# Scores head by head, the first head's mask on ScalarE, an earlier spread: one edit in a fused attention and expert kernel

## The chip, the cores and the metric

The kernel runs on one core of a Trainium2 chip. The metric is the device time of one execution in microseconds (us). Five engines work side by side, each through its own queue in program order: PE (TensorE, matrix products, whose weight loads are shown as PEld), DVE (VectorE), ACT (ScalarE), POOL (GpSimd) and SP (SyncE, which here only issues transfers). They wait for one another through semaphores.

## The reference

Attention with a threshold, then a two-layer expert, in float32:

```
scores = scale * q @ k^T                      # 8 batches x 8 heads, 576 x 576, head size 64
thresh = max(scores, axis=-1) - tau           # tau = 0.02
scores = where(scores >= thresh, scores, -1e9)
attn   = exp(scores - max); attn /= sum(attn) + 1e-9
x      = (attn @ v), heads side by side       # 4608 x 512
out    = leaky(x @ w_in) @ w_out              # leaky(h) = max(0.01 h, h); 512 -> 2048 -> 512
```

Every row of scores is needed with its maximum before anything of it can be masked, and all eight heads of a batch are needed before the expert can use a token.

## The kernel before, in words

Two heads of one batch make a pair (32 pairs), two pairs make a chunk `c` (16 chunks, two to a batch). A chunk has nine steps `t`: in steps 0 to 7 one tile of 128 queries against all 576 keys, for the two heads h = 0 and 1 of a pair; in step 8 the remaining 64 queries of both pairs. The order of all instructions is written out by hand in one loop over `c` and `t` (lines 403 to 468), and each engine executes its own in that order.

A step does the following.

- `s_mm` (L160): the scores of both heads, in PSUM, as a sum of three products of fp16 halves (hi hi, lo hi, hi lo), each in two halves of 288 keys: 12 matmuls. Head 0 uses rows 0 to 63 of the array, head 1 rows 64 to 127, and the two heads take turns. There are two PSUM buffers `s`, one for each head, so the scores of a head in the next step wait until DVE has read those of this step.
- `s_max`, once for each head (L183 to L206): DVE copies the negated scores to `sn` and takes their minimum `nmx`; POOL adds tau, which gives the threshold `nth`; ACT then does one of two things. Without `direct` it takes the exponent `e` (L193), which needs only `nmx`, and DVE masks `e` by the threshold one step later in `s_mask` (L216). With `direct` ACT masks by itself, in two instructions: `far` (L199), which needs `nth`, and `W` (L203).
- `s_mask` of the step before (L216 for each head that ACT did not mask), followed by a transposing transfer of the two weight rows on SP's queue (L222).

Around this, some steps carry more. In steps 6, 7, 8 and 0 `prep` transposes the q or k of a pair to come (L132, five matmuls into the PSUM buffer `A`), ACT copies them to fp16 `hi` (L140), and DVE makes the remainder `lo` (L141) as the last thing of the step, since it stands in the list `soon`. Between the two `s_max` of a step stand half of the step's expert units and the `prep`. After chunk c, the sums of its rows are turned into reciprocals (`sums_0` to `sums_3`, steps 0 and 1), spread over the partitions for each of its two pairs (`sums_4`: L265 into `A`, copied by ACT to `rc`, L270) and used on the product with v (`values`: 20 matmuls L281 into `A`; the product `xT`, L291, is again the last thing of DVE's step). `A` is one buffer.

The expert is cut into units of about the same size: 16 hidden units (four matmuls, L303, then ACT's `gM`, L307) and 16 parts of the output (four matmuls, L318; after every fourth ACT copies `osb`, L325) for a batch, and eight more for the last 64 tokens of two batches. `push_main` and `push_tail` put them in a list once a batch's `xT` are there; each step takes some from it: about 2.1 on average, weighted by `share[t]` over the nine steps, the fractions being carried over. A credit cannot exceed what is in the list. In chunks 0, 1 and most of 2 the list is empty; later it also runs out for two or three steps in chunks 4, 8 and 12. "The expert stage" below means everything from the first push on. The list's last 34 units are done after the loop.

POOL's queue carries, besides the thresholds, the transfers of v (5 at a time) and of the expert's weights. SP's queue carries the loads of q and k, the transposing transfers and the stores.

The line that decides who masks is in the loop:

```
direct = tau_f <= 16.0 and (
    t not in (3, 7) if c < 3 else t in (3, 5) or not any(u[0] for u in units[:n]))
s_max(c, t, 0, False)
...
s_max(c, t, 1, direct)
```

Of the kernel before, what the change touches and what calls it, by code (L numbers as in the profile page):

```python
# [16 lines left out]
def kernel(  # L17
# [52 lines left out]
    def bank():  # L70
        return ps.tile([128, 512], FP32, tag="u", bufs=2, name="u")

    def load_qk(p, i, tail):

        b, g = divmod(p, NG)
        if p not in nat:
            nat[p] = sb.tile([128, 9, 2, 64], FP32, tag="nat", bufs=3, name="nat")
        t = nat[p]
        h2 = (q, k)[i][b, 2 * g:2 * g + 2, :, :]
        if not tail:  # L80
            nc.sync.dma_start(
                out=t[0:128, 4 * i:4 * i + 4, :, :],
                in_=h2[:, 0:512, :].rearrange("h (p c) d -> p c h d", c=4),
            )
        else:
            nc.sync.dma_start(
                out=t[ds(64 * i, 64), 8, :, :],
                in_=h2[:, 512:576, :].rearrange("h p d -> p h d"),
            )
# [54 lines left out]
        ))  # L144
        qk.setdefault(p, {})[i] = (hi, lo)

    def s_mm(c, t):


        out = [ps.tile([128, 2, 512], FP32, tag="s", bufs=2, name="s") for _ in range(2)]  # L150
        if t < 8:
            srcs = [(2 * c + t // 4, ds(t % 4 * 128, 128), ds(0, 128))]
        else:
            srcs = [(2 * c + e, ds(512, 64), ds(64 * e, 64)) for e in range(2)]
        for half in range(2):
            for ti, (a, b) in enumerate(((0, 0), (1, 0), (0, 1))):
                for p, cols, po in srcs:
                    for h in range(2):
                        r = ds(h * 64, 64)
                        nc.tensor.matmul(  # L160
                            out=out[h][po, half, 0:288], lhsT=qk[p][0][a][r, cols],
                            rhs=qk[p][1][b][r, ds(half * 288, 288)],
                            start=(ti == 0), stop=(ti == 2), skip_group_check=True,
                        )
        sc[(c, t)] = out

    live, dens = {}, {}
# [86 lines left out]
    def sums_4(c, e):  # L254

        row = rows[c]
        t = pair_of_banks().rearrange("p a b -> p (a b)")

        if e == 0:
            parts = [(2 * s, s * 128, 0, 128) for s in range(4)] + [(16, 512, 0, 64)]  # L260
        else:
            parts = [(16, 0, 64, 64)] + [(8 + 2 * s, 64 + s * 128, 0, 128) for s in range(3)]
            parts += [(14, 448, 0, 64), (14, 512, 64, 64)]
        for i, q0, r0, n in parts:
            nc.tensor.matmul(  # L265
                out=t[:, ds(q0, n)], lhsT=sel[:, i:i + 2, :].rearrange("r i m -> r (i m)"),
                rhs=row[:, ds(r0, n)], start=True, stop=True, skip_group_check=True,
            )
        rc = sb.tile([128, 576], FP32, tag="rc", bufs=2, name="rc")
        nc.scalar.activation(out=rc[:, :], in_=t[:, 0:576], func=AF.Copy, bias=0.0, scale=1.0)  # L270
        rcs[e] = rc

    def values(c, e):

        b, g = divmod(2 * c + e, NG)
        wT, vb = wTs[c], Vs[b % 2]
        t = pair_of_banks()
        for half in range(2):
            for kb in range(5):
                for h in range(2):  # L280
                    nc.tensor.matmul(  # L281
                        out=t[ds(h * 64, 64), half, 0:288], lhsT=vb[:, g, h, kb, :],
                        rhs=wT[:, 4 * h + kb, ds(e * 576 + half * 288, 288)],
                        start=(kb == 0), stop=(kb == 4), skip_group_check=True,
                    )
        rc = rcs.pop(e)
        x = sb.tile([128, 576], FP16, tag=f"xT{g}", bufs=2, name=f"xT{g}")
        xTs[(b, g)] = x

        def mul():  # L290
            nc.vector.tensor_tensor(  # L291
                out=x.rearrange("p (a b) -> p a b", a=2), in0=t[:, :, 0:288],
                in1=rc.rearrange("p (a b) -> p a b", a=2), op=OP.mult,
            )
            nc.gpsimd.tensor_copy(out=xE[g][:, b, :], in_=x[:, 0:64] if e else x[:, 512:576])
        soon.append(mul)
# [76 lines left out]
            units.pop(0)[1]()  # L373

    with tc.manual_schedule():
        nc.scalar.preload_act_table_set("natural_log_exp_and_others")
        for i, tail in ((0, 0), (0, 1), (1, 1), (1, 0)):
            load_qk(0, i, tail)
        make_identity(nc, I32[:, 0:128])
        nc.vector.tensor_copy(out=I32[:, 128:192], in_=I32[:, 0:64])  # L380
        nc.vector.tensor_copy(out=I16[:, :], in_=I32[:, 0:128])
        nc.vector.memset(ntau[:, :], -tau_f)
        nc.vector.memset(r2[:, :, :], 0.0)
        nc.vector.tensor_tensor(
            out=sel[:, :, :], in0=I32[:, 0:18].unsqueeze(2).to_broadcast([128, 18, 64]),
            in1=I32[:, 64:82].unsqueeze(2).to_broadcast([128, 18, 64]), op=OP.add,
        )
        nc.vector.tensor_scalar(out=sel[:, :, :], in0=sel[:, :, :], scalar1=RS, scalar2=None, op0=OP.mult)
        for t in Vs:
            nc.vector.memset(t[64:128, :, 0, 4, :], 0.0)  # L390
            nc.vector.memset(t[0:64, :, 1, 0, :], 0.0)
        for p in range(1, 3):
            for i in range(2):
                for tail in range(2):
                    load_qk(p, i, tail)
        prep(0, 0)
        prep(0, 1, "s", 2)
        run(take(soon))
        share = (23, 27, 23, 13, 23, 13, 23, 23, 23)
        credit = 0.0  # L400
        w_at = [1 + 87 * i // 100 for i in range(32)]
        prev = None
        for c in range(NC + 1):
            last = c == NC
            for t in range(NT):
                step = c * NT + t
                if step == 1:
                    load_v(0)
                if c % 2 == 1 and t == 4 and c // 2 + 1 < B:
                    load_v(c // 2 + 1)  # L410
                for i in range(32):
                    if w_at[i] == step:
                        load_w(i)
                if c > 1 and c % 2 == 0 and t == 6:
                    push_main(c // 2 - 1)
                    if c % 4 == 0:
                        push_tail(c // 2 - 2)
                if not last:
                    s_mm(c, t)


                nxt = {6: (2 * c + 2, 0), 7: (2 * c + 2, 1), 8: (2 * c + 3, 0), 0: (2 * c + 1, 1)}
                if c == 0:
                    nxt[0], nxt[1] = (1, 0), (1, 1)
                pi = nxt.get(t)
                if pi is not None and pi[0] >= NP:
                    pi = None
                if c == 0 and t < 2:
                    prep(*pi)
                    pi = None  # L430

                if c > 0 and t in (3, 5):
                    values(c - 1, t // 2 - 1)
                credit = min(credit + 2.1 * 9 * share[t] / sum(share), len(units))
                n = int(credit)
# [69 lines left out]
```

## Time and profile before

| what | value |
|---|---|
| three runs | 554.84, 555.18 (median), 555.84 us |
| the profiled execution: its own time / its span | 553.93 us / 552.2 us |
| PE, DVE, ACT, POOL busy | 506.5, 423.1, 435.1, 183.4 us |
| mean granted clock of PE | 0.966 |
| DVE's first `sn` / that of chunk 3 / that of the last step | 10.86 / 96.62 / 498.47 us |
| DVE's copy of one head's scores (L183), 288 times | mean 752 ns |
| DVE's mask (L216), 196 times | mean 815 ns |
| ACT's exponent (L193), 196 times | mean 770 ns |
| ACT's own mask (L199 and L203), 92 times | mean 771 and 775 ns |
| POOL's threshold (L188), 288 times | mean 429 ns |

A page of the profile gives busy time by engine, then the span in 40 slices, where each digit is a busy share in tenths (PEclk is the clock granted to PE, in tenths of full speed). An instruction's duration covers its filling and emptying, so two in a row on one engine start closer together than a duration: where DVE works without a break, its copies of scores start 0.67 to 0.69 us apart. In the lists in order of time a line has its start, its length, engine, source line, operation, tiles out<-in, shapes, count, and in brackets the idle time of the engine before it with what ended that idle time.

### The profile page before, as it was taken

How to read it: one execution, taken by the hardware profiler on the slowest of the kernel's cores; microseconds unless marked ns; L12 is line 12 of the kernel's file. 1: busy time of each engine (PE TensorE's matmuls, PEld its weight loads, DVE VectorE, ACT ScalarE, POOL GpSimd, SP SyncE). 2: the span in 40 equal slices, each digit the busy share in tenths (PEclk: the TensorE clock that was granted, in tenths of full speed). 3: DMA queues.
4: the chain of work that ended last, by engine and by line, in shares of the span. 5: the costliest groups of instructions: out<-in, count | busy, mean ns of one | idle time of the engine just before them, and what ended most of it. 6: DMA issues, size and time to landing. Idle time of an engine off the chain costs nothing.

```text
span 552.2 us, 12416 instructions
## 1 busy us (share of the span) xinstructions
PE 506.5 (92%) x4416; PEld 279.6 (51%) x4416; DVE 423.1 (77%) x1106; ACT 435.1 (79%) x765; POOL 183.4 (33%) x430
## 2 busy tenths in 40 slices
PE   5668689899989999999989999999989999999996
PEld 3345445455545565455545565455545565444444
DVE  4897878798898879888898878888897878893000
ACT  2886879888987998799886998799887898885522
POOL 1756454253324222242224222242223332231000
PEclk9686859999999999999999999999999999999999
DMA  6999999999877979799867987798766976564001
GB/s 147 165 222 184 166 203 186 147 138 202 165 136 121 190 141 165 127 163 179 161 134 122 188 159 129 138 172 179 170 125 107 199 145 127 84 103 109 39 38 58
DMA packets 266814, 80.52 MB, mean 146 GB/s; under 512 B 251904, under 2 KB 264192, under 8 KB 266752
## 3 DMA queue, kind: packets, MB, share of 16 engines
q1 hardware_dynamic: 249216, 70.81, 71.3%
q0 software_dynamic: 17536, 8.92, 13.7%
q8 instruction: 35, 0.57, 0.5%
q14 instruction: 27, 0.22, 0.1%
HBM read 36.70 MB, written 9.44 MB: 84 GB/s over the span
## 4 chain that ended last, share of the span: by engine, by line
PE 53%; ACT 23%; DVE 11%; issue 7%; DMA 3%; POOL 2%; SPq 0%; DVEq 0%; ACTq 0%; POOLq 0%
PE u L318 19%; PE s L160 13%; PE u L303 11%; ACT e L193 7%; DVE sn L183 7%; PE A L281 6%; ACT gM L307 4%; ACT far L199 4%; ACT W L203 4%; PE A L132 3%; ACT hi L140 2%; DVE W L216 2%; DMA wT<-W 1%; DMA out_dram<-osb 1%; POOL nth L188 1%
## 5 line engine op out<-in xcount | busy, mean ns | idle before, releaser
L183 DVE TENSOR_SCALAR_CACHE_REDUCE sn<-s 128x576 f32<-128x576 f32 x288 | 206.9, 752 | 49.6 <-PE s L160 48.3
L188 POOL TENSOR_SCALAR nth<-nmx 128x1 f32<-128x1 f32 x288 | 123.6, 429 | 260.2 <-DVE sn L183 234.3
L193 ACT ACTIVATE e<-sn,nmx 128x576 f16<-128x576 f32 x196 | 150.5, 770 | 34.9 <-DVE sn L183 29.5
L216 DVE SCALAR_TENSOR_TENSOR W<-sn,nth,e 128x576 f16<-128x576 f32 x196 | 155.7, 815 | 2.2 <-POOL nth L188 2.2
L303 PE MATMUL u<-xT,win 128*128 128x512 f16 x512 | 128.5, 380 | 8.6 <-ACT gM L307 7.8
L318 PE MATMUL u<-wout,gM 128*128 128x512 f16 x512 | 125.3, 380 | 0.0
L160 PE MATMUL s<-hi,hi 64*128 64x288 f16 (+1 forms) x640 | 99.7, 301 | 12.6 <-DVE sn L183 11.2
L160 PEld LDWEIGHTS <-hi 64*128 64x128 f16 (+1 forms) x1280 | 67.4, 100 | 69.8 <-issue 54.3
L160 PE MATMUL s<-hi,lo 64*128 64x288 f16 (+1 forms) x640 | 94.5, 297 | 0.0
L160 PE MATMUL s<-lo,hi 64*128 64x288 f16 (+1 forms) x640 | 94.3, 297 | 0.0
L303 PEld LDWEIGHTS <-win 128*128 128x128 f16 x768 | 59.3, 98 | 67.7 <-issue 31.0
L199 ACT ACTIVATE far<-sn,nth 128x576 f32<-128x576 f32 x92 | 70.9, 771 | 23.7 <-POOL nth L188 21.5
L307 ACT ACTIVATE gM<-u 128x512 f16<-128x512 f32 x128 | 74.2, 588 | 15.8 <-PE u L303 15.8
L203 ACT ACTIVATE W<-far,ntau 128x576 f16<-128x576 f32 x92 | 71.3, 775 | 3.0
L318 PEld LDWEIGHTS <-gM 128*128 128x128 f16 x512 | 45.3, 98 | 51.1 <-issue 10.8
L141 DVE SCALAR_TENSOR_TENSOR lo<-A,hi 128x576 f16<-128x576 f32 x63 | 47.7, 757 | 23.9 <-ACT hi L140 23.6
L132 PE MATMUL A<-I,nat 128*128 128x128 f32 x315 | 49.2, 291 | 11.3 <-DVE lo L141 5.7
L132 PEld LDWEIGHTS A<-I,nat 128*128 128x128 f32 x315 | 39.2, 149 | 27.2 <-DVE lo L141 11.9
L281 PE MATMUL A<-wT,V 128*64 128x288 f16 x640 | 47.9, 298 | 1.7 <-ACT rc L270 1.6
L140 ACT ACTIVATE hi<-A 128x576 f16<-128x576 f32 x63 | 40.4, 641 | 11.5 <-PE A L132 11.5
L281 PEld LDWEIGHTS <-V 128*64 128x64 f16 x640 | 35.6, 113 | 12.7 <-issue 8.7
L160 PEld LDWEIGHTS <-lo 64*128 64x128 f16 (+1 forms) x640 | 32.9, 100 | 15.0 <-issue 11.1
(42 smaller groups left out, 279.8 us busy)
## 6 DMA issues: line engine op xcount, KB each, us to landing
nat<-in_q_dram SPq DMA_DIRECT2D x32, 256.0 KB, 4.2
nat<-in_k_dram SPq DMA_DIRECT2D x32, 256.0 KB, 3.8
out_dram<-osb SPq DMA_DIRECT2D x16, 512.0 KB, 2.9
wT<-W SPq DMA_TRANSPOSE x144, 3.9
V<-in_v_dram POOLq DMA_DIRECT2D x8, 256.0 KB, 5.6
V<-in_v_dram POOLq DMA_DIRECT2D x16, 128.0 KB, 5.8
win<-in_moe_w_in_dram POOLq DMA_DIRECT2D x16, 128.0 KB, 4.8
wout<-in_moe_w_out_dram POOLq DMA_DIRECT2D x16, 128.0 KB, 4.5
```

The lines of the kernel that those rows point to most:

```text
L132: nc.tensor.matmul(out=pt[0:128, ds(c * 128, 128)], lhsT=t[0:128, 4 * i + c if c < 4 else 8, :, :].rearrange("p h d -> p (h d)"), rhs=I32[ ...
L160: nc.tensor.matmul(out=out[h][po, half, 0:288], lhsT=qk[p][0][a][r, cols], rhs=qk[p][1][b][r, ds(half * 288, 288)], start=(ti == 0), stop= ...
L183: nc.vector.tensor_scalar(out=sn[:, h, :].rearrange("p (a b) -> p a b", a=2), in0=s_[:, :, 0:288], scalar1=-BS, scalar2=None, op0=OP.mult, ...
L188: nc.gpsimd.tensor_scalar(out=nth[:, h:h + 1], in0=nmx[:, h:h + 1], scalar1=1.0, scalar2=tau_f, op0=OP.mult, op1=OP.add,)
L193: nc.scalar.activation(out=e[:, h, :], in_=sn[:, h, :], func=AF.Exp, bias=nmx[:, h:h + 1], scale=-1.0,)
L199: nc.scalar.activation(out=far[:, :], in_=sn[:, h, :], func=AF.Prelu, bias=nth[:, h:h + 1], scale=-1.0, alpha=BIG,)
L203: nc.scalar.activation(out=w[:, ds(h * 576, 576)], in_=far[:, :], func=AF.Exp, bias=ntau[:, 0:1], scale=1.0, accum_out=dens[c][:, 2 * t + ...
L216: nc.vector.scalar_tensor_tensor(out=w[:, ds(h * 576, 576)], in0=sn[:, h, :], scalar=nth[:, h:h + 1], in1=e[:, h, :], op0=OP.is_le, op1=OP ...
L281: nc.tensor.matmul(out=t[ds(h * 64, 64), half, 0:288], lhsT=vb[:, g, h, kb, :], rhs=wT[:, 4 * h + kb, ds(e * 576 + half * 288, 288)], star ...
L303: nc.tensor.matmul(out=t[:, ts(j, N)], lhsT=w_in16[:, gi, ts(j0 + j, 128)], rhs=xs[gi], start=(gi == 0), stop=(gi == NG - 1), skip_group_c ...
L307: nc.scalar.activation(out=g_out, in_=t[:, 0:nj * N].rearrange("p (j n) -> p j n", j=nj), func=AF.Prelu, bias=0.0, scale=1.0, alpha=0.01)
L318: nc.tensor.matmul(out=t[:, :], lhsT=g_in(j), rhs=w_out16[:, j, :], start=(j == 0), stop=(j == NJ - 1), skip_group_check=True,)
```

## The change

There are five edits.

1. `s_mm` gets a flag `apart`, set when the list of units is empty at the step's start. Then all six products of head 0 come before the six of head 1; otherwise the order stays as it was.
2. `direct` now holds for head 0 instead of head 1, so ACT's queue has `far`, `W` before the units' copies and before `hi`, and `e` of head 1 after them. The steps in which ACT masks change too: in chunks 0 to 2 all but steps 2 and 7 (they were all but 3 and 7); later steps 3 and 4, and the others but step 2 if no hidden unit is among the step's units. Over the kernel that makes 87 steps with a mask on ACT (before: 92).
3. Both spreads of a chunk's sums are made in step 2 (they were made in steps 2 and 4), the second after the step's units; `values` comes in steps 3 and 4 (before: 3 and 5), behind the first half of the units.
4. The units are pushed in step 5 of an even chunk (before: 6), and `share` moves weight from steps 2 and 4 to step 5.
5. The large load of k for the first pair is issued on ACT's queue, as its first instruction. It was the fourth on SP's.

```
-        for half in range(2):
-            for ti, (a, b) in enumerate(((0, 0), (1, 0), (0, 1))):
-                for p, cols, po in srcs:
-                    for h in range(2):
...
+        if apart:
+            order = [(h, half, ti, src) for h in range(2) for ti in range(3) for half in range(2)
+                     for src in srcs]
+        else:
+            order = [(h, half, ti, src) for half in range(2) for ti in range(3) for src in srcs
+                     for h in range(2)]
...
+        load_qk(0, 1, 0, nc.scalar)
         nc.scalar.preload_act_table_set("natural_log_exp_and_others")
-        for i, tail in ((0, 0), (0, 1), (1, 1), (1, 0)):
+        for i, tail in ((0, 0), (0, 1), (1, 1)):
...
-        share = (23, 27, 23, 13, 23, 13, 23, 23, 23)
+        share = (23, 27, 21, 13, 13, 28, 23, 23, 23)
...
-                if c > 1 and c % 2 == 0 and t == 6:
+                if c > 1 and c % 2 == 0 and t == 5:
...
-                    s_mm(c, t)
+                    s_mm(c, t, not units)
...
-                if c > 0 and t in (3, 5):
-                    values(c - 1, t // 2 - 1)
...
-                        t not in (3, 7) if c < 3 else t in (3, 5) or not any(u[0] for u in units[:n]))
-                    s_max(c, t, 0, False)
+                        t not in (2, 7) if c < 3 else t in (3, 4) or t != 2 and not any(u[0] for u in units[:n]))
+                    s_max(c, t, 0, direct)
...
                 work(n - n // 2)
                 if pi is not None:
                     prep(*pi)
...
-                if c > 0 and t in (2, 4):
-                    sums_4(c - 1, t // 2 - 1)
+                if c > 0 and t == 2:
+                    sums_4(c - 1, 0)
+                if c > 0 and t in (3, 4):
+                    values(c - 1, t - 3)
                 if not last:
-                    s_max(c, t, 1, direct)
+                    s_max(c, t, 1, False)
                 work(n // 2)
+                if c > 0 and t == 2:
+                    sums_4(c - 1, 1)
```

More of the change, by code (lines that the diff above doesn't have):

```diff
@@ L71, in bank, with load_qk @@
         return ps.tile([128, 512], FP32, tag="u", bufs=2, name="u")
-    def load_qk(p, i, tail):
+    def load_qk(p, i, tail, eng=None):
+        eng = nc.sync if eng is None else eng
         b, g = divmod(p, NG)
@@ L80, in load_qk @@
         if not tail:
-            nc.sync.dma_start(
+            eng.dma_start(
                 out=t[0:128, 4 * i:4 * i + 4, :, :],
@@ L85, in load_qk @@
         else:
-            nc.sync.dma_start(
+            eng.dma_start(
                 out=t[ds(64 * i, 64), 8, :, :],
@@ L145, in prep, with s_mm @@
         qk.setdefault(p, {})[i] = (hi, lo)
-    def s_mm(c, t):
+    def s_mm(c, t, apart):
         out = [ps.tile([128, 2, 512], FP32, tag="s", bufs=2, name="s") for _ in range(2)]
@@ L154, in s_mm @@
             srcs = [(2 * c + e, ds(512, 64), ds(64 * e, 64)) for e in range(2)]
-        for half in range(2):
-            for ti, (a, b) in enumerate(((0, 0), (1, 0), (0, 1))):
-                for p, cols, po in srcs:
-                    for h in range(2):
[L159 to L164, printed above, removed]
+        terms = ((0, 0), (1, 0), (0, 1))
+        if apart:
[4 more added lines that the diff above has]
+                     for h in range(2)]
+        for h, half, ti, (p, cols, po) in order:
+            a, b = terms[ti]
+            r = ds(h * 64, 64)
+            nc.tensor.matmul(
+                out=out[h][po, half, 0:288], lhsT=qk[p][0][a][r, cols],
+                rhs=qk[p][1][b][r, ds(half * 288, 288)],
+                start=(ti == 0), stop=(ti == 2), skip_group_check=True,
+            )
         sc[(c, t)] = out
```

## The prediction

> **What bounds the kernel now.** I read the page first (busy time and slices), then the granted clock and busy time by stage, then the instructions in order of time inside single steps. "D" is a step in which ACT masks a head. T is the start of DVE's first copy of scores (L183) in a step, so a step's length is T to the next T.
>
> ```profile
> PE 506.5 (92%) x4416; PEld 279.6 (51%) x4416; DVE 423.1 (77%) x1106; ACT 435.1 (79%) x765; POOL 183.4 (33%) x430
> PE   5668689899989999999989999999989999999996
> DVE  4897878798898879888898878888897878893000
> PEclk9686859999999999999999999999999999999999
> ```
>
> The first six slices (83 us) are another regime than the rest: PE has gaps there and its clock swings. By stage, from the first L183 to chunk 3, to the last step's end, and the end:
>
> ```profile
> core 0: us, PE busy (x) PEld busy (x) DVE busy (x) ACT busy (x) POOL busy (x), PEclk, DMA share, GB/s
> 10.86:96.62 85.76, 67.65 (x558) 40.00 (x558) 74.07 (x193) 68.06 (x119) 48.22 (x104) 0.78 1.25 185
> 96.62:499.10 402.48, 387.04 (x3539) 212.52 (x3537) 340.47 (x891) 343.92 (x609) 132.71 (x314) 1.00 0.86 149
> 499.10:552.20 53.10, 47.39 (x302) 24.25 (x300) 4.26 (x12) 20.51 (x36) 1.79 (x6) 1.00 0.20 59
> ```
>
> In the middle stage PE is busy 96%: time lost on PE there is lost for good. One D step with a prep, in chunk 5 (step 7), PE and SP left out:
>
> ```profile
> 183.33 0.76 DVE L183 TENSOR_SCALAR_CACHE_REDUCE sn<-s 128x576 f32<-128x576 f32 x1
> ...
> 184.13 0.78 ACT L193 ACTIVATE e<-sn,nmx 128x576 f16<-128x576 f32 x1
> 184.25 0.19 POOL L188 TENSOR_SCALAR nth<-nmx 128x1 f32<-128x1 f32 x1 [2.38 <-DVE sn L183]
> ...
> 184.69 0.81 DVE L216 SCALAR_TENSOR_TENSOR W<-sn,nth,e 128x576 f16<-128x576 f32 x1
> 184.85 0.65 ACT L140 ACTIVATE hi<-A 128x576 f16<-128x576 f32 x1
> ...
> 185.53 0.76 DVE L141 SCALAR_TENSOR_TENSOR lo<-A,hi 128x576 f16<-128x576 f32 x1
> 185.59 0.78 ACT L199 ACTIVATE far<-sn,nth 128x576 f32<-128x576 f32 x1
> ...
> 186.40 0.78 ACT L203 ACTIVATE W<-far,ntau 128x576 f16<-128x576 f32 x1
> ...
> 186.58 0.76 DVE L183 TENSOR_SCALAR_CACHE_REDUCE sn<-s 128x576 f32<-128x576 f32 x1 [0.29 <-PE s L160]
> ```
>
> To be seen: ACT does e, then hi, and only then far and W. So hi ends at T+2.17, just when DVE is through with two copies and a mask (T+2.10), and lo follows without a wait worth listing. The step takes 3.25 and is PE's: its scores, two units and transposes start at 182.39 and come round at 185.60, 3.21 later. When hi is late, DVE stands still, as in chunk 1, step 6, which began at 55.81:
>
> ```profile
> 58.71 0.63 ACT L140 ACTIVATE hi<-A 128x576 f16<-128x576 f32 x1
> ...
> 59.37 0.76 DVE L141 SCALAR_TENSOR_TENSOR lo<-A,hi 128x576 f16<-128x576 f32 x1 [1.38 <-ACT hi L140]
> ...
> 60.05 0.75 DVE L183 TENSOR_SCALAR_CACHE_REDUCE sn<-s 128x576 f32<-128x576 f32 x1
> ```
>
> That step took 4.24: the copy of scores queued behind lo begins only when lo has gone through.
>
> **D steps with a prep (edit 2).** With head 0 masked by ACT, the order on ACT is far, W, hi, e. A ring then closes inside one step: L183 to the next start on DVE 0.68; read-out and threshold 0.46 (184.01 to 184.25, then 0.19, then 0.03 to ACT); far to W 0.80 (from 57.27-56.48 to 186.40-185.59); W to the next ACT start 0.78 (57.27 to 58.05); hi 0.66 with its signal; lo to the next L183 0.68 (59.37 to 60.05). Sum 4.06, whatever PE does. A copy of units (0.5 back to back) standing between W and hi adds to it. Running through the order of the code there are 32 such steps: 0, 6, 8 of the first chunks (8 in all) and 6, 7, 8 and the next 0 in chunks 3 to 14 (24). Eight of the 24 have an osb copy before hi, two of the eight a gM.
> In the trace the same 24 steps take 83.5 us (six groups of four, 13.5 to 14.2 each), with as many units in them as after. They become 24 x 4.06 + 8 x 0.5 = 101.4: **+17.9**. The eight early ones take 27.2 and become 8 x 4.06 + 1.0, and 0.3 for chunk 1, step 6, where v's transfers (3.3 on POOL) delay a threshold: 33.8, **+6.6**. What this buys is small: far waits for the quick threshold (0.19, beside the copy of head 1) rather than the slow one (0.70, beside the mask), but ACT's idle time before far is 21.5 us in all and mostly not on the path.
>
> **Scores in turn (edit 1).** A lone head uses half the array. A 512-column matmul on the whole array follows the last by 216 ns, so 288 columns cost 0.12; twelve in a row 1.44 instead of 0.84 (182.39 to 183.23). Bounds: 0.84 (nothing lost) and 12 x 0.24 = 2.9 at half clock (20.46 to 22.1 shows six pairs 0.24 apart). The gain is that head 0's scores are made while DVE still copies head 1. At full clock DVE then never waits: 2 x 0.68 + 0.74 = 2.1 for a D step without prep, against 2.3 to 2.9 now; 2.83 with two masks. By this the other 19 steps up to chunk 3 become 55.9 us, from 58.6: chunk 0 from 19.8 to 18.9 (its first two slower by 1.0, since PE is at half clock and does 2.9 plus 1.3 of transposes each, the rest faster), chunk 1 18.9 to 17.4, chunk 2 19.9 to 19.6 although it does three units more. **-2.7**, and **-2.6** for these units (0.87 each) which later stages need not do.
> The Trainium skill, "TensorE: Matmul & The Clock Gate", Part 3 (what overlaps), says that a weight load overlaps running matmuls only when the row group differs. By that, each of a lone head's loads (100 ns) would add to its 0.12 and a step's scores cost 2.6. The trace does not bear it out: L303's matmuls, all on the same rows, each with its own load, follow at 216 ns, the bare streaming time. I keep 1.44.
>
> **Start (edit 5).** q's transposes hold PE to 5.84; k's began at 6.58, when its load landed, 0.74 later. k issued 2.2 earlier lands in time (bounds 0 and 0.74). Head 0 need not wait for the buffer that lo of k frees (the second matmul waits from 8.65 to 9.44), so the first L183 comes at 9.65: **-1.2**. SP's later loads move up 0.65; ACT's table load (1.28) moves back 0.7 and is covered until 5.87.
>
> **Spreads and values (edits 3 and 4).** In step 2 the second spread waits until ACT has copied the first out of A: ACT does e, gM, rc, about T+2.6, while PE is free at T+2.0. That step becomes 3.75 (2.9 to 4.1 now). Step 3 has two masks and xT on DVE, 3.5, step 4 2.8, as steps 3 to 5 now. Added up for an odd chunk's steps 0 to 5 with the same 12 units: 21.5 against 21.6 to 22.1; for an even chunk's steps 1 to 8: 0.1 more in three, 0.2 in one, 1.3 in two. Seven odd by -0.3 and six even by +3.1 in all: **+1.0**, bounds -8 (a third of the 24 us that these 93 steps, 319 us, hold beyond PE's own work of 295) and +5. Push and share move units by a step and change no count.
> At the end, the first spread, rc, second spread, values, xT, values, xT run with three units less between them: waits of 0.9, 0.9, 1.0 and 0.3 on PE against 1.2 + 0.5 now: **+1.4** (0 to 3).
>
> **Sum:** 17.9 + 6.6 - 2.7 - 2.6 - 1.2 + 1.0 + 1.4 = +20.4, on the profiled execution's 553.93 (span 552.2): 574.3. It lies 1.25 under the median shown, which I leave inside the rounding: **574**.
>
> **The rivals.** (a) *The ring does not bind and the early stage decides: faster.* If hi were not held up, the 32 steps would stay at 110.7 and the early stage would lose all of DVE's waits: DVE's own work in chunk 0 to 2's step 4 is 23.8 + 24.7 + 13.9, 9.4 under the time taken, and 1.2 at the start: 554 - 10.6 = 543. For it: PE is 96% busy in the middle, DVE only 85%, and DVE waits 40 us there for scores, so much of its delay is usually free. Against it: after 4.06 PE has nothing left to do, its next scores needing the buffers that L183 frees and its next transposes the A that lo frees. The switch is at a mean of 3.5 us for the 32 steps (3.46 now): below it the change gains.
> (b) *Half of it is caught up.* ACT drains its backlog in the ring's pauses and the steps between reach the lower bounds (-8, early -4): 562.
> (c) *PE's clock falls in the early stage,* as it does now: stretches with PE busy 1.88 of 3.41 us (36.33 to 39.74) went over to half clock, 2.76 of 3.42 (80.70 to 84.12) did not. A D step with prep is busy 2.0 of 4.06, the others 1.44 of 2.1. If it falls half the time, six steps go from 2.1 or 2.25 to 2.9: 578. The skill's same page, Part 1, has activity release the throttle in windows of about 3.4 us, and by it denser scores stay at full clock; the trace's changes of clock, 3.4 or 10.2 us apart, agree, and the sum above assumes it.
>
> **How the numbers follow.** The forecast 574 (566 to 580) 0.62; (a) 0.18; (b) 0.12; (c) 0.08. Under 0.2% (1.1 us, about what this measurement can tell) only the tails between (a) and (b) fall: 0.02. So faster 0.18, same 0.02, slower 0.80. The range leaves out most of (a) and the top of (c): 548 to 580.
>
> **What would show it.** In the profile after: lo (L142) waiting for hi over 1 us in the D steps with prep, some 32 times and over 40 us in all (24.9 now); those steps at 4.06 or 4.55; PE busy about 93% instead of 96% in the middle stage, waiting for DVE's sn or lo. Right on the early stage: chunk 3's first L183 near 99, with 23 units in the list. It is wrong if these steps stay at 3.2 to 3.6, or if the first 80 us shrink by 5 or more.

## The result

The changed kernel takes 602.54 us (median of four runs, 602.06 to 602.76). On the same chip the kernel before takes 555.51 us (554.84 to 555.90, four runs), so the ratio is 1.0847 with an interval of 1.0828 to 1.0866: 47.0 us slower. The direction was forecast, the size was not. 574 was given, and the time lies 22.5 us above the range.

From the page of the changed kernel, busy time by engine, PE's slices, the granted clock, and the shares of the chain that ended last:

```profile
PE 520.3 (87%) x4416; PEld 288.1 (48%) x4416; DVE 425.8 (71%) x1116; ACT 428.3 (71%) x755; POOL 174.6 (29%) x430
PE   5778688897899889898898889998898879999896
PEclk9767759999999999999999999999899999999999
...
ACT 35%; PE 23%; DVE 17%; issue 12%; POOL 6%; DMA 5%; DVEq 0%; POOLq 0%; SPq 0%; ACTq 0%
```

The last row in the kernel before:

```profile
PE 53%; ACT 23%; DVE 11%; issue 7%; DMA 3%; POOL 2%; SPq 0%; DVEq 0%; ACTq 0%; POOLq 0%
```

No engine does much more work than before (PE 506.5 to 520.3, DVE 423.1 to 425.8, ACT 435.1 to 428.3), and all of them idle more. PE's nines between slice 7 and the end have become eights and nines. In the chain PE had 53% before and has 23% now; ACT went from 23% to 35%. This is time spent waiting in a chain from engine to engine, not work.

By stage (first copy of scores to chunk 3, to the last step's copy, to the end; the columns are the stretch, its length, then busy time and count for each engine):

```profile
core 0: us, PE busy (x) PEld busy (x) DVE busy (x) ACT busy (x) POOL busy (x), PEclk, DMA share, GB/s
10.36:107.60 97.24, 76.67 (x573) 46.24 (x571) 74.95 (x194) 70.34 (x124) 46.83 (x104) 0.75 1.10 167
107.60:546.80 439.20, 393.15 (x3530) 214.54 (x3531) 341.65 (x900) 334.13 (x593) 125.23 (x314) 1.00 0.77 135
546.80:600.60 53.80, 46.49 (x296) 24.02 (x295) 4.97 (x12) 21.20 (x38) 1.79 (x6) 0.99 0.23 61
```

The middle stage grew from 402 to 439 us with the clock at 1.00 in both, and PE is busy 393.15/439.20 = 89.5% of it, from 96%. The last step's copy is the boundary here (498.5 before). The four parts of the span against what the prediction's sum gives for each:

| part | before | predicted | after | after less predicted |
|---|---|---|---|---|
| to the first `sn` copy | 10.86 | 9.65 | 10.36 | +0.7 |
| from there to chunk 3 | 85.8 | 89.7 | 97.2 | +7.5 |
| chunk 3 to the last step's copy | 401.8 | 419.8 | 439.2 | +19.4 |
| end | 53.7 | 53.4 | 53.8 | +0.4 |

(89.7 is 33.8 + 55.9; 419.8 is 401.8 + 17.9 + 1.0 - 0.9; 53.4 is 53.7 + 1.4 - 1.7. The three units' 2.6 are put where the traces have them: 1061 matmuls of the expert start in the middle stage, against 1065 before, which is one unit less, and 243 at the end, against 251, which is two.) The last column adds up to 28.0, the whole miss.

What DVE waited for in the changed kernel (total us, times, longest us):

```profile
DVE lo L142 <- ACT hi L141: 51.3, 46, 3.3
DVE sn L190 <- PE s L167: 49.3, 51, 2.2
DVE W L223 <- issue: 18.7, 7, 3.9
```

The first is the ring that the prediction described. It was 24.9 us before. The third was not foreseen. One of the seven waits is at the end of the kernel (1.9); the other six, 2.4 to 3.9 each, are in step 5 of the odd chunks 3 to 13, one step after each load of v. That of chunk 1 (2.6) is put down to the threshold itself, in another row.

The ring, in the changed kernel's list in order of time, chunk 5, step 8, from one copy of head 0's scores to the next:

```profile
206.62 0.75 DVE L190 TENSOR_SCALAR_CACHE_REDUCE sn<-s 128x576 f32<-128x576 f32 x1
...
207.56 0.19 POOL L195 TENSOR_SCALAR nth<-nmx 128x1 f32<-128x1 f32 x1 [3.29 <-DVE sn L190]
...
207.78 0.78 ACT L206 ACTIVATE far<-sn,nth 128x576 f32<-128x576 f32 x1 [1.21 <-POOL nth L195]
...
208.59 0.78 ACT L210 ACTIVATE W<-far,ntau 128x576 f16<-128x576 f32 x1
...
209.36 0.63 ACT L141 ACTIVATE hi<-A 128x576 f16<-128x576 f32 x1
...
210.02 0.76 DVE L142 SCALAR_TENSOR_TENSOR lo<-A,hi 128x576 f16<-128x576 f32 x1 [1.23 <-ACT hi L141]
...
210.69 0.75 DVE L190 TENSOR_SCALAR_CACHE_REDUCE sn<-s 128x576 f32<-128x576 f32 x1
...
210.83 0.76 PE L133 MATMUL A<-I,nat 128*128 128x128 f32 x5 [0.64 <-DVE lo L142]
```

From 206.62 to 210.69 is 4.07, where the prediction had 4.06. `hi` starts only after `far` and `W`, `lo` starts 0.66 after `hi`, and the next copy stands behind `lo` on DVE. PE, too, stands: its next transposes need the `A` that `lo` frees.

The second delay, same kernel and chunk, steps 4 and 5:

```profile
190.14 0.24 POOL L302 COPY xE<-xT 128x64 f16<-128x64 f16 x1 [1.43 <-DVE xT L298]
...
190.62 3.27 POOL L96 DMA_DIRECT2D V<-in_v_dram  x5 [0.25 <-issue]
...
193.97 0.45 POOL L195 TENSOR_SCALAR nth<-nmx 128x1 f32<-128x1 f32 x2
...
194.19 0.78 ACT L206 ACTIVATE far<-sn,nth 128x576 f32<-128x576 f32 x1 [4.22 <-POOL nth L195]
...
195.00 0.78 ACT L210 ACTIVATE W<-far,ntau 128x576 f16<-128x576 f32 x1
...
195.77 0.76 ACT L200 ACTIVATE e<-sn,nmx 128x576 f16<-128x576 f32 x1
...
196.62 0.82 DVE L223 SCALAR_TENSOR_TENSOR W<-sn,nth,e 128x576 f16<-128x576 f32 x1 [2.38 <-issue]
```

POOL works in the order of its queue. The five transfers of v stand behind the copy `xE`, which waits for step 3's `xT`, and ahead of step 4's two thresholds. The thresholds are made at 193.97, though the copy of scores that head 0's needs began at 189.99. ACT sits idle for 4.22 because, with head 0's mask on ACT in step 4, `far` waits for that threshold, and `W` and head 1's `e` stand behind `far`. DVE's mask waits for that `e`. Its cause is the threshold, though the row puts the wait down to "issue". The same three things stand in the same order on POOL in the kernel before (its list, chunk 5, steps 4 and 5):

```profile
173.43 0.24 POOL L295 COPY xE<-xT 128x64 f16<-128x64 f16 x1 [1.43 <-DVE xT L291]
173.91 3.27 POOL L95 DMA_DIRECT2D V<-in_v_dram  x5 [0.25 <-PE u L303]
177.26 1.85 POOL L188 TENSOR_SCALAR nth<-nmx 128x1 f32<-128x1 f32 x4
...
179.14 0.77 ACT L199 ACTIVATE far<-sn,nth 128x576 f32<-128x576 f32 x1 [1.71 <-POOL nth L188]
```

There ACT masks nothing in step 4. The late thresholds are needed by DVE a step later (0.18 of waiting), and by the `far` of step 5's second head, which is the last of its step.

### The profile page after: what moved, and what is told of

The parts are those of the page before. It is cut to its first block, busy times and chain, and to the rows that moved or that the text cites. A ratio compares the mean times of both kernels' runs of the same rounds, so it can differ in the third digit from the quotient of the medians.

```text
span 600.6 us, 12404 instructions
## 1 busy us (share of the span) xinstructions
PE 520.3 (87%) x4416; PEld 288.1 (48%) x4416; DVE 425.8 (71%) x1116; ACT 428.3 (71%) x755; POOL 174.6 (29%) x430
## 3 DMA queue, kind: packets, MB, share of 16 engines
q0 software_dynamic: 17536, 8.92, 12.9%
## 4 chain that ended last, share of the span: by engine, by line
ACT 35%; PE 23%; DVE 17%; issue 12%; POOL 6%; DMA 5%; DVEq 0%; POOLq 0%; SPq 0%; ACTq 0%
DVE sn L190 11%; ACT e L200 10%; ACT far L206 7%; PE s L167 7%; ACT W L210 7%; PE u L310 6%; PE u L325 5%; ACT gM L314 4%; DVE W L223 4%; ACT hi L141 4%; DMA wT<-W 3%; PE A L288 3%; POOL V L96 3%; POOL nth L195 2%; DMA nat<-in_q_dram 2%
## 5 line engine op out<-in xcount | busy, mean ns | idle before, releaser
L190 DVE TENSOR_SCALAR_CACHE_REDUCE sn<-s 128x576 f32<-128x576 f32 x288 | 206.3, 750 | 49.9 <-PE s L167 49.3
L195 POOL TENSOR_SCALAR nth<-nmx 128x1 f32<-128x1 f32 x288 | 114.8, 399 | 317.5 <-DVE sn L190 307.2
L200 ACT ACTIVATE e<-sn,nmx 128x576 f16<-128x576 f32 x201 | 154.2, 769 | 32.1 <-DVE sn L190 27.8
L223 DVE SCALAR_TENSOR_TENSOR W<-sn,nth,e 128x576 f16<-128x576 f32 x201 | 159.4, 814 | 24.9 <-issue 18.7
L206 ACT ACTIVATE far<-sn,nth 128x576 f32<-128x576 f32 x87 | 67.2, 773 | 91.9 <-POOL nth L195 91.7
L325 PE MATMUL u<-wout,gM 128*128 128x512 f16 x512 | 123.9, 380 | 0.0
L167 PE MATMUL s<-hi,hi 64*128 64x288 f16 (+1 forms) x640 | 97.1, 303 | 10.5 <-DVE sn L190 9.8
L167 PEld LDWEIGHTS <-hi 64*128 64x128 f16 (+1 forms) x1280 | 69.7, 100 | 67.4 <-issue 52.1
L142 DVE SCALAR_TENSOR_TENSOR lo<-A,hi 128x576 f16<-128x576 f32 x63 | 47.6, 756 | 51.1 <-ACT hi L141 51.0
L133 PE MATMUL A<-I,nat 128*128 128x128 f32 x315 | 51.0, 297 | 25.5 <-DVE lo L142 19.9
L210 ACT ACTIVATE W<-far,ntau 128x576 f16<-128x576 f32 x87 | 67.4, 775 | 2.8
L133 PEld LDWEIGHTS A<-I,nat 128*128 128x128 f32 x315 | 39.5, 151 | 45.0 <-DVE lo L142 30.9
L288 PEld LDWEIGHTS <-V 128*64 128x64 f16 x640 | 36.0, 115 | 17.3 <-issue 13.3
L167 PEld LDWEIGHTS <-lo 64*128 64x128 f16 (+1 forms) x640 | 38.3, 103 | 10.0 <-issue 2.2
```

The source lines that it names most:

```text
L133: nc.tensor.matmul(out=pt[0:128, ds(c * 128, 128)], lhsT=t[0:128, 4 * i + c if c < 4 else 8, :, :].rearrange("p h d -> p (h d)"), rhs=I32[ ...
L167: nc.tensor.matmul(out=out[h][po, half, 0:288], lhsT=qk[p][0][a][r, cols], rhs=qk[p][1][b][r, ds(half * 288, 288)], start=(ti == 0), stop= ...
L190: nc.vector.tensor_scalar(out=sn[:, h, :].rearrange("p (a b) -> p a b", a=2), in0=s_[:, :, 0:288], scalar1=-BS, scalar2=None, op0=OP.mult, ...
L195: nc.gpsimd.tensor_scalar(out=nth[:, h:h + 1], in0=nmx[:, h:h + 1], scalar1=1.0, scalar2=tau_f, op0=OP.mult, op1=OP.add,)
L200: nc.scalar.activation(out=e[:, h, :], in_=sn[:, h, :], func=AF.Exp, bias=nmx[:, h:h + 1], scale=-1.0,)
L206: nc.scalar.activation(out=far[:, :], in_=sn[:, h, :], func=AF.Prelu, bias=nth[:, h:h + 1], scale=-1.0, alpha=BIG,)
```

## The experiments

The theory at the outset was the prediction's: the ring, made by `far` and `W` of head 0 standing ahead of `hi`. Its rivals were the second spread in step 2, the clock or the order of the scores in the early stage, and later v's transfers on POOL. No experiment leaves out any computation. To compare steps, three sums from the traces are used: "ring steps" are the 24 steps of the middle stage that have a mask on ACT and a prep in the changed kernel (the kernel before has three more such steps, left out of its sum), "early ring steps" the 8 before chunk 3, and "v steps" step 5 of the seven odd chunks that load v. A step goes from its first copy of scores to the next one's. The ratios are against the kernel before on the same chip, whose median was 553.5 to 555.5 there; differences between the times of two kernels are good to about 2 us.

| kernel | ratio to before (95%) | ring steps | early ring steps | v steps | step 2 of chunks 1 to 15 |
|---|---|---|---|---|---|
| before | 1 | 83.5 | 27.2 | 26.5 | 48.4 |
| after | 1.0847 (1.0828 to 1.0866) | 105.5 | 35.1 | 34.6 | 60.3 |
| a_head1 | 1.0289 (1.0251 to 1.0327) | 87.1 | 29.8 | 23.9 | 62.8 |
| b_head0 | 1.0696 (1.0629 to 1.0764) | 104.5 | 34.1 | 31.7 | 49.0 |
| a_prep_first | 1.0531 (1.0493 to 1.0570) | 87.5 | 27.0 | 35.2 | 61.4 |
| a_turns | 1.0899 (1.0852 to 1.0945) | 105.5 | 35.1 | 34.6 | 60.3 |
| b_apart_k | 1.0019 (0.9980 to 1.0058) | 83.5 | 28.2 | 26.8 | 47.6 |
| b_spread2 | 1.0351 (1.0294 to 1.0409) | 83.5 | 27.7 | 25.6 | 60.5 |
| a_v_early | 1.0633 (1.0564 to 1.0702) | 102.7 | 36.2 | 23.3 | 60.3 |
| b_apart_k_v | 0.9959 (0.9927 to 0.9991) | 85.3 | 26.6 | 23.8 | 47.8 |
| a_prep_v | 1.0302 (1.0262 to 1.0342) | 83.6 | 28.2 | 23.3 | 61.3 |
| b_head0_prep_v | 1.0228 (1.0188 to 1.0267) | 88.5 | 26.0 | 25.6 | 47.8 |
| a_ring_off | 1.0354 (1.0320 to 1.0388) | 81.8 | 27.9 | 34.7 | 61.5 |
| b_mixed_v | 1.0045 (1.0017 to 1.0073) | 85.1 | 26.1 | 23.9 | 48.1 |

**The changed kernel with ACT masking head 1 again (a_head1).**

```
-                    s_max(c, t, 0, direct)
+                    s_max(c, t, 0, False)
...
-                    s_max(c, t, 1, False)
+                    s_max(c, t, 1, direct)
```

> The changed kernel, but ACT masks head 1 again (far and W after hi). Ring theory (hi behind far and W holds lo and with it the next step's copy of scores): the 32 masked steps with a prep fall from 140.7 us to about 112, and the steps after v's transfers, which wait for a late threshold, lose another 8: 566 us (560 to 572). Rival, the other edits cost the time: it stays above 585.

569.90 us. Putting the mask back on head 1 gives back 32.6 us of the 47.0. The ring steps fall from 105.5 to 87.1, and the v steps from 34.6 to 23.9, so both delays hang on it. The second is not gone altogether: step 6 of the odd chunks 3 to 13, right after, still has a mean of 4.66 (4.69 in the changed kernel, 3.38 before), since the late mask now makes ACT late for step 6. Over the six chunks that is 7.7 us. Step 2 stays long (62.8), and 15.9 us over the kernel before remain.

**The kernel before with the mask on head 0 (b_head0).**

```
-                    s_max(c, t, 0, False)
+                    s_max(c, t, 0, direct)
...
-                    s_max(c, t, 1, direct)
+                    s_max(c, t, 1, False)
```

> The kernel before with one edit: ACT masks head 0 instead of head 1, in the same steps. Ring theory: the 32 steps with a prep go to 4.1 to 4.7 each, so 555 becomes 585 us (578 to 592). Rival, the other edits cost the time: within 5 us of 555.

592.68 us, just above the range expected. The swap alone, in the steps of the kernel before, costs 7% (6.3 to 7.6), with the ring steps at 104.5. The ring does not need the rest of the change. The ring steps and the early ring steps are 27.9 of its 38.6 us, so head 0 on ACT costs something in other steps too (the v steps have 31.7, from 26.5).

**The changed kernel with the prep ahead of the first mask (a_prep_first).** Here `hi` goes to ACT's queue ahead of `far`.

```
+                    if pi is not None:
+                        prep(*pi)
...
                     s_max(c, t, 0, direct)
...
                 work(n - n // 2)
-                if pi is not None:
-                    prep(*pi)
```

> The changed kernel, ACT still masking head 0, but the prep (transposes and hi) is put ahead of the first head's work, so that hi stands before far and W on ACT. Ring theory: lo no longer waits, the masked steps with a prep go back to 3.2 to 3.7, while the steps after v's transfers stay slow: 573 us (566 to 582). Rival, masking head 0 is slow in itself (far waits for a threshold wherever hi stands): above 590.

583.45 us, 19.1 less, and 1.5 above the range expected. Its waits of DVE (total, times, longest):

```profile
DVE sn L190 <- PE s L167: 75.6, 71, 4.4
...
DVE lo L142 <- ACT hi L141: 5.2, 5, 3.1
```

The wait for `hi` is all but gone (51.3 to 5.2), and the ring steps are 87.5. Part of the gain came back as waits for scores, 49.3 to 75.6, since the transposes now stand ahead of the units on PE and nothing fills the time until `hi` is copied. So the ring costs at least what this run gives back.

**The changed kernel with the heads always taking turns (a_turns).**

```
-                    s_mm(c, t, not units)
+                    s_mm(c, t, False)
```

> The changed kernel with the two heads' scores always in turns as before (edit 1 undone). Prediction's theory: scores head by head were worth 2 to 3 us, so 605 us (601 to 608). Rival: twice the PE time at half clock in the first 100 us cost more than they gave, 597 us or less.

603.77 us against 602.54: scores head by head are worth 1.2 us in the changed kernel, less than the ratios can tell. The early stage is 98.5 instead of 97.2. The order of the scores is not where the time went.

**The kernel before with scores head by head and k on ACT's queue (b_apart_k).** Edits 1 and 5 alone.

```
+        load_qk(0, 1, 0, nc.scalar)
...
-        for i, tail in ((0, 0), (0, 1), (1, 1), (1, 0)):
+        for i, tail in ((0, 0), (0, 1), (1, 1)):
...
-                    s_mm(c, t)
+                    s_mm(c, t, not units)
```

> The kernel before with edits 1 and 5 alone (scores head by head while no units are waiting; k of the first pair on ACT's queue). My theory after the first four runs: the 15 us that the changed kernel keeps when ACT masks head 1 come from the two spreads in step 2, so without them little is left: 553 us (550 to 556), the first copy of scores 0.5 earlier. Rival, scores head by head cost the time (twice the PE work, PE longer at half clock in the first 100 us): 560 or more.

555.16 us, ratio 1.0019 (0.9980 to 1.0058): no difference that can be measured. The first copy of scores comes at 10.38 instead of 10.86, which is 0.5 of the 1.2 predicted. From there to chunk 3 it takes 85.7, against 85.8.

**The kernel before with both spreads in step 2 (b_spread2).** The values stay in steps 3 and 5.

```
-                if c > 0 and t in (2, 4):
-                    sums_4(c - 1, t // 2 - 1)
+                if c > 0 and t == 2:
+                    sums_4(c - 1, 0)
...
                 work(n // 2)
+                if c > 0 and t == 2:
+                    sums_4(c - 1, 1)
```

> The kernel before with one part of edit 3: both spreads of a chunk in step 2, values still in steps 3 and 5. Theory: PE's second spread waits for ACT's copy of the first, and the next step's scores stand behind it on PE; 1 to 2 us in each of the 15 chunks that have spreads beside scores, some of it given back where the second spread stood: 555 plus 8 to 15 us. Rival, the step is PE-bound or DVE-bound anyway and the wait is free: within 3 us of 555.

574.04 us, 3.5% slower (2.9 to 4.1): 20.2 us, more than the 8 to 15 expected. Step 2 goes from 48.4 to 60.5 over chunks 1 to 15, and step 3 of chunks 3 to 15 from 49.1 to 58.8. Its list in order of time, chunk 6, steps 2 and 3:

```profile
202.78 0.63 ACT L270 ACTIVATE rc<-A 128x576 f32<-128x576 f32 x1
...
203.45 0.41 PE L265 MATMUL A<-row,sel 128*128 128x64 f16 x6 [0.22 <-ACT rc L270]
...
204.74 0.76 DVE L183 TENSOR_SCALAR_CACHE_REDUCE sn<-s 128x576 f32<-128x576 f32 x1 [1.38 <-PE s L160]
...
205.50 0.64 ACT L270 ACTIVATE rc<-A 128x576 f32<-128x576 f32 x1
...
206.19 0.56 PE L281 MATMUL A<-wT,V 128*64 128x288 f16 x6 [1.48 <-ACT rc L270]
```

The second spread waits on PE until ACT has copied the first out of `A`. The next scores stand behind it on PE, so DVE waits 1.38 for them. The second `rc` stands behind `far`, `W` and a copy of units on ACT, and PE's `values` wait 1.48 for it. The prediction named the first of these two waits, not the second.

**The changed kernel with v loaded two steps earlier (a_v_early).** In step 2 ACT masks nothing, so a late threshold holds up no `far`.

```
-                if c % 2 == 1 and t == 4 and c // 2 + 1 < B:
+                if c % 2 == 1 and t == 2 and c // 2 + 1 < B:
```

> The changed kernel with v's five transfers issued in step 2 of the odd chunks instead of step 4, a step in which ACT does not mask, so that no threshold that ACT waits for stands behind them on POOL. Theory: step 5 of chunks 1, 3, 5 ... 13 loses 1.1 to 2.4 us each, 9 us in all: 593 us (590 to 596). Rival, the long step 5 comes from its three units: 602.

589.30 us, 13.2 less than the changed kernel, where 9 was expected. The v steps go from 34.6 to 23.3, and DVE's wait put down to "issue" from 18.7 to 1.9. Its list in the same place of chunk 5, POOL and the head of ACT's mask:

```profile
190.31 0.24 POOL L302 COPY xE<-xT 128x64 f16<-128x64 f16 x1 [0.69 <-DVE xT L298]
...
191.13 0.19 POOL L195 TENSOR_SCALAR nth<-nmx 128x1 f32<-128x1 f32 x1 [0.58 <-DVE sn L190]
...
191.35 0.78 ACT L206 ACTIVATE far<-sn,nth 128x576 f32<-128x576 f32 x1 [0.47 <-POOL nth L195]
```

With the transfers gone from between them, `far` waits 0.47 for its threshold, not 4.22. The wait for `hi` stays at 51.3 us: the two delays are separate.

**The kernel before with edits 1 and 5 and an earlier v (b_apart_k_v).** b_apart_k, and:

```
-                if c % 2 == 1 and t == 4 and c // 2 + 1 < B:
+                if c % 2 == 1 and t == (3 if c == 1 else 2) and c // 2 + 1 < B:
```

> The kernel before with edits 1 and 5 and with v's transfers issued in steps in which ACT does not mask (step 3 of chunk 1, step 2 of the later odd chunks). If the wait for thresholds behind v's transfers costs the kernel before anything, 1 to 4 us under the run with edits 1 and 5 alone, and below 555; if not, the same as that run.

551.48 us, ratio 0.9959 (0.9927 to 0.9991). It is faster than both kernels, than the kernel before by 0.1 to 0.7%. Part of the delay by v was in the kernel before as well: the v steps go from 26.5 to 23.8. The ring steps take most of that back (83.5 to 85.3), and the middle stage gives 1 us (401.8 to 400.8); the start gives 0.6, and the early stage takes 0.6 more (86.4). Against b_apart_k the medians differ by 3.7 us and the profiled spans by only 0.3 (551.4 and 551.1); the times of b_apart_k lie between 552.4 and 559.4, and where the rest of its 3.7 us went is not shown.

**The changed kernel with both cures, prep first and v early (a_prep_v).** The two diffs of a_prep_first and a_v_early together.

> The changed kernel with both waits of its masked steps taken away, ACT still masking head 0: prep ahead of the first head's work, v's transfers in step 2. If the two are separate costs they add up: 602.5 - 19 - 13 = 570 us (567 to 574), the same as with head 1 masked, and what is left over the kernel before is the two spreads in step 2. Rival, the two overlap: 576 or more.

570.79 us. From a_prep_first it is 12.7 less, as a_v_early was 13.2 less than the changed kernel: the two add up. What remains over before, 17.3 us, contains hardly any wait for `hi` (5.0 us) and no late threshold (v steps 23.3). Step 2 is at 61.3, 12.9 above before, and DVE waited 84.7 us for scores (48.3 before).

**The best kernel with head 0's mask and the prep ahead of it (b_head0_prep_v).** b_apart_k_v, the swap of b_head0, and `prep` moved as in a_prep_first.

> The kernel before with edits 1 and 5, v's transfers in steps without a mask on ACT, and head 0 masked by ACT with prep ahead of the first head's work: every edit of the change that is left once its three waits are avoided. If it does not matter which head ACT masks: 551 us (549 to 554), like the same kernel with head 1. If the quicker threshold of head 0 is worth something: below 549. If prep right behind the scores makes PE wait for the buffer that lo frees: 556 or more.

566.72 us, ratio 1.0228 (1.0188 to 1.0267), 15 us above b_apart_k_v. The early ring steps are as short as anywhere (26.0), but the ring steps are 88.5 and step 3 of chunks 3 to 15 takes 52.1 instead of 49.1. DVE waited 78.2 us for scores (46.6 in b_apart_k_v). So head 0 on ACT does not become free when `hi` is put ahead. b_mixed_v, below, puts 5.8 of the 15 us on head 0 in steps 1 to 5. The rest comes with head 0 and the moved transposes in the prep steps, and no run tells these two apart.

**The changed kernel with head 0 masked only where there is no prep (a_ring_off).** In steps 6, 7, 8 and 0 ACT masks head 1.

```
-                    s_max(c, t, 0, direct)
+                    s_max(c, t, 0, direct and 0 < t < 6)
...
-                    s_max(c, t, 1, False)
+                    s_max(c, t, 1, direct and not 0 < t < 6)
```

> The changed kernel, but in the steps that may carry a prep (6, 7, 8 and 0) ACT masks head 1; in steps 1 to 5 it masks head 0 as before. Ring theory: just these steps get short, 24 of them from 105.6 to about 85 us and the 8 early ones from 35 to 29, while the steps after v's transfers stay long: 602.5 - 27 = 576 us (571 to 580). Rival, the head's place matters in all steps alike: about 590.

573.93 us, 28.6 less than the changed kernel. This is the cleanest price of the ring: 23.7 us in the ring steps and 7.2 in the early ones, 30.9 of steps, of which the other steps take 2.5 back. Its list in order of time, chunk 5, step 6, shows the order restored on ACT, and `lo` with little to wait for:

```profile
190.14 0.63 ACT L141 ACTIVATE hi<-A 128x576 f16<-128x576 f32 x1
...
190.68 0.77 ACT L206 ACTIVATE far<-sn,nth 128x576 f32<-128x576 f32 x1
...
190.81 0.76 DVE L142 SCALAR_TENSOR_TENSOR lo<-A,hi 128x576 f16<-128x576 f32 x1 [0.32 <-ACT hi L141]
```

The v steps stay at 34.7: head 0 is still masked by ACT in step 4.

**The best kernel with head 0 masked only where there is no prep (b_mixed_v).** b_apart_k_v, with

```
-                    s_max(c, t, 0, False)
+                    s_max(c, t, 0, direct and 0 < t < 6)
...
-                    s_max(c, t, 1, direct)
+                    s_max(c, t, 1, direct and not 0 < t < 6)
```

> The kernel before with edits 1 and 5 and v's transfers moved, ACT masking head 0 in steps 1 to 5 and head 1 in the others. If the quicker threshold is worth anything where no prep follows: below 550. If not: 551.5 as with head 1 everywhere (549.5 to 553.5).

557.29 us, 5.8 above b_apart_k_v (4.8 by the ratios) and above both times expected. Even without a prep in the step and without v in the way, masking the first head gains nothing. Its list, chunk 6, step 2:

```profile
197.41 0.78 ACT L206 ACTIVATE far<-sn,nth 128x576 f32<-128x576 f32 x1 [0.49 <-POOL nth L195]
...
198.22 0.78 ACT L210 ACTIVATE W<-far,ntau 128x576 f16<-128x576 f32 x1
...
198.99 0.63 ACT L277 ACTIVATE rc<-A 128x576 f32<-128x576 f32 x1
...
199.67 1.42 PE L288 MATMUL A<-wT,V 128*64 128x288 f16 x20 [0.52 <-ACT rc L277]
```

It is the same pattern with another victim: `rc` stands behind `far` and `W`, and PE's `values` wait for it. Step 3 of chunks 3 to 15 has 52.1 here too, against 49.1 in the kernel before.

## Why the prediction was right and wrong

**The ring (edit 2) was right, in place and size.** The ring steps were to be 101.4; they are 105.5, and 102.7 where v is out of the way. In chunk 5, step 8 takes 4.07 and step 7, with another copy ahead of `hi`, 4.57 (4.06 and 4.55 predicted). Step 6 takes 4.69 without such a copy, since the late mask of step 5 still holds ACT up; with v out of the way it takes 4.07. The next step 0 takes 4.25, since a small reciprocal stands in it as well. The early ones were to be 33.8 and are 35.1. `lo` waited 51.3 us, over the 40 forecast, in 46 waits. Rival (a) had all 32 steps unchanged at 110.7, and they take 140.6. Rival (b) had half of it caught up in the other steps, and those became longer.

**"With as many units in them as after" was wrong.** Of the six groups of four steps, four held ten units before and two held nine; after, all six hold nine. With the ring binding whatever PE does, the four missing units have to be done in other steps, where PE has to find time for them. At the prediction's 0.87 a unit that is 4 x 0.87 = 3.5 us that the sum left out. This is worked out from the order of the code, and no run isolates it.

**The wait for thresholds behind v's transfers was the step that failed most: 0.3 was allowed for it, and it took 13.** With it failed the term for the middle stage outside the ring, which had +1.0 for edits 3 and 4 with +5 as the bound, and nothing for v. These steps went from 318.3 to 333.7, and with the 1.0 and one unit's 0.9 less they should be 318.4, so 15.3 too little was allowed. Of that,

- v's transfers are 8.7 (333.7 against 325.0 in a_v_early), and 2.8 more in the ring steps. With 1.5 in the early stage the whole is 13.0 of the span, and 13.2 of the time. The prediction knew the 3.3 us on POOL, and allowed 0.3, in chunk 1's step 6 alone. Two facts that it had were not put together: after edit 2 ACT masks in steps 3 and 4, no longer 3 and 5, and v is loaded in step 4; and with head 0 the mask has the step's other `e` behind it. The same queue that cost little before stands on the path now.
- the four missing units are 3.5.
- the remainder, 15.3 - 8.7 - 3.5 = 3.1, is about what the two spreads in step 2 cost beyond the estimate of 3.75 a step: step 2 of chunks 3 to 15 takes 51.5, where 13 x 3.75 = 48.8 (42.6 before, with eight units more). Alone, on the kernel before, the two spreads cost 20.2 us (574.04 against 553.87 on the same chip); there step 2 of these chunks takes 51.5 as well, and step 3 grows from 49.1 to 58.8. In the whole change step 3 takes 46.2, with its values moved and ten units fewer in it. In chunk 5 step 2 takes 4.00; the early steps 2 of chunks 1 and 2, without units, take 4.39.

**The early stage: predicted 89.7, measured 97.2.** The eight ring steps account for 1.3. The other 19 were to take 55.9 and take 62.2. Of these 6.3, v's transfers are 2.7 (59.5 in a_v_early, where the ring steps take 1.1 more). Another 1.6 is gain that edit 1 did not bring: b_apart_k, without ring or second spread in step 2, has 57.5 (85.7 - 28.2), where 58.6 was before and 55.9 was predicted. The two spreads make step 2 of chunks 1 and 2 longer, 4.39 each from 2.92, which is more than the 2.0 that are left. Rival (c), a falling clock, is there in part: between 10 and 100 us the mean granted clock is 0.79 before, 0.73 after and 0.77 in a_v_early. It goes with the delays more than with the scores, for a_ring_off and b_apart_k, both with scores head by head, have 0.79. (In the trace before, the changes of clock lie 3.4, 10.2 and once 13.7 us apart, not only 3.4 or 10.2.) The Trainium skill, "TensorE: Matmul & The Clock Gate", Part 1, has activity release the throttle, and the prediction read that as a reason why denser scores keep the clock up. In b_apart_k PE was busier than before (77.6 us of these 90, against 70.9) at the same clock; a_turns has 0.70, against the changed kernel's 0.73. So the runs neither show it nor rule it out. What the clock cost in the changed kernel was not measured by itself.

**The price of a lone head's scores was right.** The list of the changed kernel in an early step, each row two matmuls of 288 columns:

```profile
62.65 0.40 PE L167 MATMUL s<-hi,hi 64*128 64x288 f16 x2 [2.49 <-DVE sn L190]
...
62.89 0.40 PE L167 MATMUL s<-hi,lo 64*128 64x288 f16 x2
...
63.13 0.42 PE L167 MATMUL s<-lo,hi 64*128 64x288 f16 x2
...
63.72 0.68 PE L167 MATMUL s<-hi,lo 64*128 64x288 f16 x2
...
64.20 0.68 PE L167 MATMUL s<-lo,hi 64*128 64x288 f16 x2
```

Starts are 0.24 apart for two at first, 0.12 each, and 0.48 for two once the clock has fallen. By the granted clock of the two stretches (same columns as the stages above) that is full and half speed:

```profile
62.60:63.30 0.70, 0.65 (x6) 0.47 (x6) 0.67 (x2) 0.70 (x2) 0.18 (x1) 1.00 1.57 190
63.40:66.00 2.60, 1.48 (x8) 0.61 (x5) 1.39 (x3) 2.56 (x5) 0.72 (x2) 0.50 1.24 212
```

So the prediction's 1.44 and 2.9 for twelve both hold. The rule of the Trainium skill's same page, Part 3, by which a weight load overlaps running matmuls only in another row group, would have made it 0.22 for each; the trace does not show that. The gain hoped for, 2.7 us over 19 steps, did not come: a_turns and b_apart_k put it at about 1 us and at nothing that can be measured. Some early steps did become short (2.35 to 2.45 in the changed kernel), but the kernel's first two, where PE is at half clock, became longer.

**Start and end.** The first copy came 0.5 earlier, not 1.2: head 0's scores have `lo` of k as an operand, and that was made from 8.71 to 9.47, so the products that need it came after it. The prediction freed them from the buffer that this `lo` releases, and forgot the operand. The end took 53.8, 0.1 more than before, with two units (1.7) less to do; so its waits grew by 1.8 where 1.4 was allowed.

**The ledger in whole runs.** Of 47.0 us the ring is 28.6 (a_ring_off), v's transfers 13.2 (a_v_early), and 5.2 remain for the spreads, the moved units and the clock, if the first two add up (by the ratios, 4.9% of 554 us is 27.3 for the ring and 2.1% is 11.9 for v, and 7.7 remain). For the prep-first cure that addition was run; for a_ring_off together with the earlier v it was not, and no run has edit 4 alone.

## What to carry to other kernels

When an operation that waits for another engine is moved up in a queue, list what stands behind it there, and ask of each who needs it next. Here `hi`, `e` and `rc` all stood behind one pair of mask instructions, and each was on another engine's path. Look also at the queue that it waits for: transfers issued on POOL are work in that queue, and a threshold of 0.19 us behind 3.27 us of them costs whatever the waiting engine holds up. And when a step becomes bound by a ring, the work that PE could have done in it is not free elsewhere, so count the units in both kernels, not in one.

## What was not expected of the hardware

A transfer of v holds POOL's queue for 0.63 to 0.92 us each (40 of them, median 0.65 in the changed kernel) before anything behind it starts. The clock changed only at points that lie 3.41 us or a multiple of it apart. Cut along that grid, the traces before and after have eight stretches up to 100 us that ran at full clock with PE busy 0.92 to 1.88 of 3.41 us, and half clock came behind each of them; behind the others at full clock, with 2.07 or more, it did not. One pause was enough: the 2.49 us that PE stood before the scores at 62.65 shown above lie in the stretch with 0.92, which ends at 63.39. The bound is not the same in every kernel: in b_apart_k half clock also came behind stretches with 1.89 to 2.24. And a mean granted clock of 0.79 in the early stage was the same with PE busy 70.9 and 77.6 of 90 us.
